# A fused attention and feed-forward kernel: the hidden tile of the seven-product blocks is taken from attention's four accumulator banks, and a probability buffer becomes a second copy of hs

## The chip, the cores and the metric

The kernel runs on one core of a Trainium2 chip. The metric is the time on the device in microseconds, the median of the runs shown. A core has five engines that matter here: TensorE (PE, matmuls, with its weight loads as PEld), VectorE (DVE), ScalarE (ACT), GpSimd (POOL) and SyncE (SP, which issues the transfers). Matmuls write into eight accumulator banks (PSUM), which VectorE and ScalarE read; this kernel's whole arrangement turns on who holds which bank.

## The reference

Eight heads of 64 and eight batches. Each of 512 local queries sees the 32 global keys and the local keys within 32 positions; each of 32 global queries sees all 544 keys. The 4608 rows that come out, 512 wide, go through a feed-forward pair with an ELU between:

```python
s_ll = where(abs(pos[:, None] - pos[None, :]) <= 32, scale * q_l @ k_l.T, -1e9)
a_l  = softmax(concat([scale * q_l @ k_g.T, s_ll]))        # local queries
out  = concat([softmax(scale * q_g @ k_all.T) @ v_all, a_l @ concat([v_g, v_l])])
x    = out.transpose(0, 2, 1, 3).reshape(4608, 512)
h    = x @ w_in                                            # 512 -> 2048
g    = where(h > 0, h, exp(min(h, 0)) - 1)
y    = g @ w_out                                           # 2048 -> 512
```

## The kernel before

**Two streams.** `attention()` and `ffn_stream()` are generators that are woven together: the last loop of `attn_ffn` draws stages of attention one by one and, after each, as many steps of the feed-forward stream as `pace` asks for. A `yield` ends a step; `tick` counts them, and `defer(n, fn)` writes an instruction into the program n ticks later. This gives the program's order. A planner then sorts the instructions into each engine's queue by that order as priority and by its own model of durations, and gives each tile of a pool a buffer as one comes free. On the chip each engine runs its queue in that fixed order and waits by semaphores.

**The banks.** Three pools divide the eight banks: `ps_h` (two, tiles h), `ps_o` (two, tiles acc) and `ps_a` (four, tiles pa).

**Attention.** A slot is one tile of 128 queries of four heads (64 such tiles, two groups g by four tiles t for each of eight batches), or the global queries of a batch and group (`stage_ga`). `stage_s` makes scores in two pa banks (L768), adds the mask and takes the extremum on VectorE (L779, into the buffer p), and defers the exponential (L785, ScalarE) and the scaling (L792, GpSimd). Two slots later `stage_t` transposes p (L808) into a pa bank, which line 810 copies out, and `stage_u` transposes global parts (L741, L744) into another, which lines 745 to 749 copy out. `stage_vv` multiplies by the values (L888, L821) into two banks for two tiles at a time; ScalarE (L896) and VectorE (L901) read them. From the third batch on, three slots after its first (`switch` in the code), a slot's stages come in the order T, S, U, V; before that S, V, T, U. The buffers p were a rotation of `LAGT + 1` = 3.

**Feed-forward.** The rows of x are taken in 18 blocks of 256. Weights and activations are split into a high and a low float16, and each product is three matmuls. Early blocks run in parts, as the weights' groups a to d become ready, with plain products (L445) in the acc banks. Once all weights are in (group f), a block's second layer is made by seven products of quarters in the manner of Strassen (`ffn2_seven`, L481), which need four accumulators for the eight pairs p of a block. Such a job carries a list, `seven`, which is None for the plain blocks.

`ffn1(job, p)` makes h for one pair: 24 matmuls (L322) into one bank. ScalarE reads h twice, as g (L331, Relu) and hs (L332, Copy), then takes the exponential of g (L333). VectorE joins g and hs (L340), for seven-product blocks four ticks later, and adds quarters (L354 to L356); ScalarE makes the high half gh (L359), VectorE the low half gl (L343). The second layer of a pair runs two pairs later (`LAG2`). At a block's end ScalarE evacuates the four accumulators (L491, L493). `ffn1_last` and `sums_of_last` do the same in smaller pieces for the very last pair.

**What sets h's bank before.** h comes from the two banks of `ps_h`. The first call of `ffn2_seven` takes four accumulators for the rest of the run: both acc, one h and one pa. From then on one bank is left for h and three for attention. When attention's stages are all issued (`alone`), every second h comes from `ps_a`. hs has one buffer.

Of the kernel before, what the change touches and what calls it, by code (L numbers as in the profile page):

```python
# [10 lines left out]
F32 = mybir.dt.float32  # L11
# [10 lines left out]
DM, DF = 512, 2048  # L22
P = 128
NT = SL // P
HQ = P // 2
KW = HQ + 3 * 32
# [34 lines left out]
def attn_ffn(ctx: ExitStack, tc: tile.TileContext, qT, qgT, kT, vT, vgT, vpT, w_in, w_out, mask, out):  # L61
# [35 lines left out]
            tick()  # L97

    lead = [True]
    alone = [False]  # L100


    msk = wts.tile([P, 3, KW], F32, name="msk")
# [7 lines left out]
    def clear(p):  # L111
        nc.gpsimd.memset(p[HQ:P, 0, :], 0.0)
        nc.gpsimd.memset(p[0:HQ, 1, :], 0.0)

    for p in ptw[:2]:
        clear(p)
    pkd = [wts.tile([P, P], F32, name=f"pk{i}") for i in range(2)]
    for p in pkd:
        nc.gpsimd.memset(p, 0.0)

# [182 lines left out]
    def ffn_stream():  # L303
# [3 lines left out]
        def ffn1(job, p):  # L307
            group, blk, xh, xl, sc, seven = job
            if (blk, p) == (order[-1], NP - 1):
                yield from ffn1_last(job, p)  # L310
                return
            state["h"] = not state.get("h")
            if alone[0] and state["h"]:
                h = ps_a.tile([P, 512], F32, name="pa").rearrange("p (j t) -> p j t", j=2)
            else:
                h = ps_h.tile([P, 2, BLK], F32, name="h")
            for j in range(2):
                f = slice((2 * p + j) * P, (2 * p + j + 1) * P)
                k = 0
                for c in range(NC):  # L320
                    for wt, xt in ((win[0], xh), (win[0], xl), (win[1], xh)):
                        nc.tensor.matmul(h[:, j, :], wt[:, c, f], xt[:, c, :], start=k == 0, stop=k == 11)  # L322
                        k += 1
                        if k == 6:
                            yield
                if j == 0:
                    yield
            g = ffn.tile([P, 2 * BLK], F32, name="g", bufs=2)
            hs = ffn.tile([P, 2 * BLK], F32, name="hs", bufs=1)
            hf = h.rearrange("p j t -> p (j t)")  # L330
            nc.scalar.activation(g, hf, AF.Relu, scale=sc[:, p:p + 1])  # L331
            nc.scalar.activation(hs, hf, AF.Copy, scale=sc[:, 2 * NP + 1 + p:2 * NP + 2 + p])  # L332
            nc.scalar.activation(g, g, AF.Exp, scale=-1.0)  # L333
            sg = sc[:, NP + p:NP + p + 1]
            shape = [P, 2 * BLK] if seven is None else [P, 7, P]
            gh = ffn.tile(shape, F16, name="gh", bufs=3)
            gl = ffn.tile(shape, F16, name="gl", bufs=3)

            def elu(out, *ins):
                nc.vector.scalar_tensor_tensor(out=out, in0=ins[0], scalar=-1.0, in1=ins[1], op0=ALU.add, op1=ALU.max)  # L340

            def low(dst, src, hi):
                nc.vector.scalar_tensor_tensor(out=dst, in0=src, scalar=sg, in1=hi, op0=ALU.mult, op1=ALU.subtract)  # L343

            def plain():
                elu(g, g, hs)
                nc.scalar.activation(gh, g, AF.Copy, scale=sg)
                defer(1, lambda: low(gl, g, gh))

            def parts():  # L350

                gx, q = quarters()
                elu(q, *(a.rearrange("p (a x) -> p a x", x=P) for a in (g, hs)))
                nc.vector.tensor_add(gx[:, 2:4, :], q[:, 0:2], q[:, 2:4])  # L354
                nc.vector.tensor_sub(gx[:, 5:7, :], q[:, 0:4:2], q[:, 1:4:2])
                nc.vector.tensor_add(gx[:, 0, :], q[:, 1], q[:, 2])  # L356

                def high():
                    nc.scalar.activation(gh, gx, AF.Copy, scale=sg)  # L359

                def lows():
                    low(gl, gx, gh)
                    seven.append(p)

                defer(2, high)
                defer(4, lows)

            defer(*(2, plain) if seven is None else (4, parts))
            pend.append((job, p, gh, gl))
            yield  # L370
# [7 lines left out]
        def ffn1_last(job, p):  # L378

            _, _, xh, xl, sc, seven = job  # L380
            g = ffn.tile([P, 2 * BLK], F32, name="g", bufs=2)
            hs = ffn.tile([P, 2 * BLK], F32, name="hs", bufs=1)
            s = new_x()[0].rearrange("p c (a x) -> p (c a) x", x=P)
            gh, gl = (ffn.tile([P, 7, P], F16, name=n, bufs=3) for n in ("gh", "gl"))
            q = g.rearrange("p (a x) -> p a x", x=P)
            sg = sc[:, NP + p:NP + p + 1]

            def parts(a, src):
                nc.scalar.activation(gh[:, a, :], src, AF.Copy, scale=sg)
                nc.vector.scalar_tensor_tensor(out=gl[:, a, :], in0=src, scalar=sg, in1=gh[:, a, :],  # L390
                                               op0=ALU.mult, op1=ALU.subtract)

            for j in range(2):
                h = ps_a.tile([P, 512], F32, name="pa")[:, 0:BLK]
                f = slice((2 * p + j) * P, (2 * p + j + 1) * P)
                k = 0
                for c in range(NC):
                    for wt, xt in ((win[0], xh), (win[0], xl), (win[1], xh)):
                        nc.tensor.matmul(h, wt[:, c, f], xt[:, c, :], start=k == 0, stop=k == 11)
                        k += 1  # L400
                        if k == 6:
                            yield
                gj, hj = (a[:, j * BLK:(j + 1) * BLK] for a in (g, hs))
                nc.scalar.activation(gj, h, AF.Relu, scale=sc[:, p:p + 1])
                nc.vector.tensor_scalar(hj, h, sc[:, 2 * NP + 1 + p:2 * NP + 2 + p], 1.0, ALU.mult, ALU.mult)
                nc.scalar.activation(gj, gj, AF.Exp, scale=-1.0)
                nc.vector.scalar_tensor_tensor(out=gj, in0=gj, scalar=-1.0, in1=hj, op0=ALU.add, op1=ALU.max)
                if j == 0:
                    nc.vector.tensor_sub(s[:, 5, :], q[:, 0], q[:, 1])
                    parts(1, q[:, 1])  # L410
                    parts(5, s[:, 5, :])
                    yield
            nc.vector.tensor_add(s[:, 2:4, :], q[:, 0:2], q[:, 2:4])
            parts(slice(2, 4), s[:, 2:4, :])
            nc.vector.tensor_sub(s[:, 6, :], q[:, 2], q[:, 3])
            nc.vector.tensor_add(s[:, 0, :], q[:, 1], q[:, 2])
            parts(4, q[:, 2])
            parts(0, s[:, 0, :])
            parts(6, s[:, 6, :])
            seven.append(p)  # L420
            pend.append((job, p, gh, gl))
            yield
# [38 lines left out]
        def ffn2_seven(blk, steps, sc, done):  # L461

            if "seven" not in state:
                state["seven"] = [ps_o.tile([P, DM], F32, name="acc"), ps_o.tile([P, DM], F32, name="acc"),
                                  ps_h.tile([P, 2, BLK], F32, name="h").rearrange("p a b -> p (a b)"),
                                  ps_a.tile([P, 512], F32, name="pa")]
            acc = state["seven"]
            oc = sc[:, 2 * NP:2 * NP + 1]
            final = blk == order[-1]
# [189 lines left out]
    def attention():  # L659
# [95 lines left out]
        def stage_s(st, g, t):  # L755
# [14 lines left out]
            mi = 0 if t == 0 else (2 if t == NT - 1 else 1)  # L770
            m = apool.tile([P, 4], F32, name="m", bufs=3)
            s = apool.tile([P, 2, 4], F32, name="sm", bufs=3)
            pp = apool.tile([P, 4, KW], F32, name="p", bufs=LAGT + 1)
            ps = [pp[:, i, :] for i in range(4)]
            np_[0] += 4
            for i in (0, 2, 1, 3):
# [171 lines left out]
        for i in range(n + LAGT + 1):  # L948
# [6 lines left out]
                load_values(s1)  # L955
            if i == switch:
                clear(ptw[2])
            for what in "SVTU" if i < switch else "TSUV":
                if what in "TU" and s1 and s1[0] == "l":
                    (stage_t if what == "T" else stage_u)(sts[s1[1]], *s1[2:])  # L960
                elif what == "V" and i < switch:
                    if s2 and s2[0] == "l":
                        stage_v(sts[s2[1]], *s2[2:])
                    if s0 and s0[1] < PAIRED:
                        load_values(s0)
                elif what == "V":
                    if pairs:
                        b, g, half = pairs.pop()
                        stage_vv(sts[b], g, half)
                    if s1 and s1[0] == "l" and s1[3] % 2 == 1:  # L970
                        pairs.append((s1[1], s1[2], s1[3] // 2))
                elif what == "S" and s0 and s0[0] == "g":
                    stage_ga(sts[s0[1]], s0[2])
                elif what == "S" and s0:
                    stage_s(sts[s0[1]], *s0[2:])
                yield
# [19 lines left out]
    for i, _ in enumerate(attention()):  # L996
# [10 lines left out]
        while done < want:  # L1007
# [3 lines left out]
            done += 1  # L1011
            convert(1)
            tick()
    alone[0] = True
    for _ in f:
        tick()
    drain()
# [52 lines left out]
```

## Time and profile before

| what | us |
|---|---|
| median of 3 runs (lowest to highest) | 968.35 (965.91 to 968.85) |
| the profiled execution, its own time | 968.7 |
| its span, first to last instruction | 966.9 |
| TensorE busy (mean granted clock 0.981) | 908.5 |
| VectorE busy | 739.7 |
| ScalarE busy | 662.7 |
| GpSimd busy | 271.2 |
| first h of a plain block (L322) | 84.6 |
| first and last start of a seven-product matmul (L481) | 332.9 and 961.1 |
| last matmuls of attention (L821) | 834.4 |

The table is read from the page, which gives engines as busy time, and from the views of single lines, which give first and last start. In the views below a row of the waits reads: engine and line that waited, what ended the wait, microseconds in total, times, the longest. A row of the timeline reads: start, duration, engine, line, operation, output and inputs, shapes, and in brackets the idle time of the engine before it and what ended that. A row of the groups ends with busy time, mean nanoseconds of one, and idle time of the engine ahead of them. A matmul's end is modelled and lies past the start of the next one, so a row's idle time is counted from there.

### The profile page before, as it was taken

Reading aid. Unit: us, or ns where it says so; the run is one execution under the profiler, and the core shown is the slowest. Engines: PE = TensorE matmul, PEld = TensorE weight load, DVE = VectorE, ACT = ScalarE, POOL = GpSimd, SP = SyncE. Lnnn points to the kernel's source line nnn. Section 1 sums busy time; section 2 is a strip of 40 time slices with the busy share of each in tenths; the row PEclk is TensorE's granted clock in tenths of the full one; section 3 lists DMA queues with packets and bytes.
Section 4 is the critical chain, followed back from the end, with each engine's and each line's share of the span. In section 5 each row is a group of like instructions: output and inputs, shape, how many; then the busy total and the mean of one; then the engine's idle time right before and its main releaser. Section 6 shows DMA issues by size and latency. Waiting matters only on the chain.

```text
span 966.9 us, 23599 instructions
## 1 busy us (share of the span) xinstructions
PE 908.5 (94%) x9216; PEld 725.6 (75%) x9216; DVE 739.7 (76%) x2033; ACT 662.7 (69%) x1568; POOL 271.2 (28%) x483
## 2 busy tenths in 40 slices
PE   5778988799999999999999999999999999999997
PEld 2546565466667788788888888888888788888886
DVE  4978999989957777768777777686777767676565
ACT  4767887776665777658676767676766767666564
POOL 3647193370532222122121212221322222110000
PEclk8899999999999999999999999999999999999999
DMA  7853765530343023101230123102310101000000
GB/s 268 287 173 129 254 221 197 185 118 37 120 138 119 25 99 100 47 26 45 100 124 26 45 78 123 45 27 83 115 48 25 45 24 34 1 23 23 1 23 22
DMA packets 41767, 87.61 MB, mean 91 GB/s; under 512 B 7736, under 2 KB 8888, under 8 KB 41656
## 3 DMA queue, kind: packets, MB, share of 16 engines
q1 hardware_dynamic: 41368, 85.85, 26.2%
q8 instruction: 72, 1.18, 0.5%
q14 instruction: 39, 0.32, 0.1%
q10 hardware_dynamic: 288, 0.26, 0.1%
HBM read 70.89 MB, written 15.20 MB: 89 GB/s over the span
## 4 chain that ended last, share of the span: by engine, by line
PE 59%; ACT 15%; DVE 15%; DMA 5%; issue 3%; POOL 2%; SPq 0%; DVEq 0%; ACTq 0%
PE h L322 23%; PE acc L481 10%; PE h L481 5%; PE acc L445 4%; PE pa L821 3%; PE pa L322 3%; ACT p L785 3%; PE pa L768 2%; DMA raw<-w_out 2%; PE pa L481 2%; ACT gh L359 2%; PE pa L808 2%; ACT g L331 2%; ACT hs L332 2%; DVE gl L343 2%
## 5 line engine op out<-in xcount | busy, mean ns | idle before, releaser
L322 PE MATMUL h<-xh,winh 128*128 128x256 f16 x984 | 269.3, 274 | 11.1 <-ACT hs L332 10.7
L322 PE MATMUL h<-xl,winh 128*128 128x256 f16 x984 | 269.0, 273 | 0.5 <-DVE xl L570 0.5
L322 PE MATMUL h<-xh,winl 128*128 128x256 f16 x984 | 269.0, 273 | 0.0
L322 PEld LDWEIGHTS <-winh 128*128 128x128 f16 x2160 | 209.2, 98 | 49.7 <-issue 19.2
L792 POOL TENSOR_SCALAR p<-p,sm 128x128 f32<-128x128 f32 x256 | 144.5, 580 | 319.4 <-DVE sm L790 198.3
L359 ACT ACTIVATE gh<-gx,xs 128x896 f16<-128x896 f32 x103 | 107.3, 1042 | 122.3 <-DVE gx L356 122.2
L343 DVE SCALAR_TENSOR_TENSOR gl<-gx,xs,gh 128x896 f16<-128x896 f32 x103 | 119.4, 1160 | 60.3 <-ACT gh L359 59.3
L481 PEld LDWEIGHTS <-gh 128*128 128x128 f16 x1456 | 139.6, 98 | 22.8 <-issue 6.2
L785 ACT ACTIVATE p<-p,m 128x160 f32<-128x160 f32 x256 | 106.6, 419 | 41.5 <-DVE m L779 41.3
L340 DVE SCALAR_TENSOR_TENSOR gx<-g,hs 128x512 f32<-128x512 f32 x103 | 72.8, 706 | 71.4 <-ACT g L333 70.0
L322 PEld LDWEIGHTS <-winl 128*128 128x128 f16 x1080 | 106.0, 98 | 14.0 <-issue 1.0
L331 ACT ACTIVATE g<-h,xs 128x512 f32<-128x512 f32 x123 | 84.0, 683 | 42.3 <-PE h L322 41.7
L481 PE MATMUL acc<-wouth,gh 128*128 128x256 f16 x312 | 85.2, 273 | 0.0
L333 ACT ACTIVATE g<-g 128x512 f32<-128x512 f32 x135 | 85.0, 630 | 0.0
L481 PE MATMUL acc<-woutl,gh 128*128 128x256 f16 x312 | 85.0, 273 | 0.0
L481 PE MATMUL acc<-wouth,gl 128*128 128x256 f16 x312 | 85.0, 273 | 0.0
L332 ACT ACTIVATE hs<-h,xs 128x512 f32<-128x512 f32 x123 | 83.8, 682 | 0.0
L481 PEld LDWEIGHTS <-gl 128*128 128x128 f16 x728 | 71.2, 98 | 9.3 <-DVE gl L343 1.0
L779 DVE CUSTOM_DVE_ANT_0 p<-pa,msk 128x160 f32<-128x160 f32 x228 | 61.1, 318 | 6.4 <-PE pa L768 6.2
L768 PE MATMUL pa<-k,q 64*64 64x160 f32 x912 | 51.4, 315 | 6.0 <-ACT ptg L749 5.3
L445 PE MATMUL acc<-wouth,gh 128*128 128x512 f16 x128 | 49.6, 388 | 7.3 <-DVE o L453 4.8
L808 PE MATMUL pa<-ident,p 128*128 128x128 f32 x256 | 43.9, 284 | 11.2 <-POOL p L792 9.6
(236 smaller groups left out, 1897.4 us busy)
## 6 DMA issues: line engine op xcount, KB each, us to landing
k<-kT SPq DMA_DIRECT2D x32, 640.0 KB, 5.1
v<-vT SPq DMA_DIRECT2D x64, 256.0 KB, 2.8
q<-qT SPq DMA_DIRECT2D x32, 256.0 KB, 5.5
raw<-w_in SPq DMA_DIRECT2D x8, 1024.0 KB, 7.0
raw<-w_out SPq DMA_DIRECT2D x8, 1024.0 KB, 6.1
out<-o SPq DMA_DIRECT2D x32, 256.0 KB, 2.3
od<-o SPq DMA_DIRECT2D x24, 256.0 KB, 3.1
o<-od SPq DMA_DIRECT2D x24, 256.0 KB, 2.8
```

Of the source, the lines that this page charges most:

```text
L322: nc.tensor.matmul(h[:, j, :], wt[:, c, f], xt[:, c, :], start=k == 0, stop=k == 11)
L331: nc.scalar.activation(g, hf, AF.Relu, scale=sc[:, p:p + 1])
L332: nc.scalar.activation(hs, hf, AF.Copy, scale=sc[:, 2 * NP + 1 + p:2 * NP + 2 + p])
L333: nc.scalar.activation(g, g, AF.Exp, scale=-1.0)
L340: nc.vector.scalar_tensor_tensor(out=out, in0=ins[0], scalar=-1.0, in1=ins[1], op0=ALU.add, op1=ALU.max)
L343: nc.vector.scalar_tensor_tensor(out=dst, in0=src, scalar=sg, in1=hi, op0=ALU.mult, op1=ALU.subtract)
L359: nc.scalar.activation(gh, gx, AF.Copy, scale=sg)
L445: nc.tensor.matmul(acc[t], gt[:, s], wt[:, f, :], start=p == first and j == 0 and k == 0, stop=p == last and j == 1 and k == 2)
L481: nc.tensor.matmul(cols, gt, w, start=p == 0 and k == 0, stop=last and k == len(todo) - 1, skip_group_check=True)
L768: nc.tensor.matmul(sp[r][half * HQ:(half + 1) * HQ, j * KW:(j + 1) * KW], q[rows, qs], k[rows, t, half, :], start=True, stop=True)
L785: nc.scalar.activation(ps[i], ps[i], AF.Exp, bias=m[:, i:i + 1], scale=-1.0, accum_out=s[:, 0, i:i + 1])
L792: nc.gpsimd.tensor_scalar(ps[i][:, 0:P], ps[i][:, 0:P], s[:, 1, i:i + 1], 1.0, ALU.mult, ALU.mult)
```

## The change

- h of a job with seven products comes from `ps_a`, always; h of a plain job comes from `ps_h`, always. The switch by `alone` and the alternation are gone.
- The four lasting accumulators of the seven products are both acc banks and both h banks; `ps_a` keeps its four.
- The three buffers of probabilities p become named tiles that are taken in turn (`turn`), and so does hs. At `switch` the oldest of the three leaves the rotation, and 512 of its 640 columns become a second hs. From there p has two buffers and hs has two; before it p has three and hs one.

```diff
-    alone = [False]
...
+    pps = [wts.tile([P, 4, KW], F32, name=f"p{i}") for i in range(LAGT + 1)]
+    hss = [wts.tile([P, 2 * BLK], F32, name="hs")]
+    turns = {"p": 0, "hs": 0}
+
+    def turn(name, tiles):
+        turns[name] += 1
+        return tiles[turns[name] % len(tiles)]
...
-            state["h"] = not state.get("h")
-            if alone[0] and state["h"]:
+            if seven is not None:
                 h = ps_a.tile([P, 512], F32, name="pa").rearrange("p (j t) -> p j t", j=2)
             else:
                 h = ps_h.tile([P, 2, BLK], F32, name="h")
...
-            hs = ffn.tile([P, 2 * BLK], F32, name="hs", bufs=1)
+            hs = turn("hs", hss)
...
-                state["seven"] = [ps_o.tile([P, DM], F32, name="acc"), ps_o.tile([P, DM], F32, name="acc"),
-                                  ps_h.tile([P, 2, BLK], F32, name="h").rearrange("p a b -> p (a b)"),
-                                  ps_a.tile([P, 512], F32, name="pa")]
+                state["seven"] = [ps_o.tile([P, DM], F32, name="acc") for _ in range(2)]
+                state["seven"] += [ps_h.tile([P, 2, BLK], F32, name="h").rearrange("p a b -> p (a b)") for _ in range(2)]
...
-            pp = apool.tile([P, 4, KW], F32, name="p", bufs=LAGT + 1)
+            pp = turn("p", pps)
...
             if i == switch:
                 clear(ptw[2])
+                k = turns["p"]
+                spare, *two = (pps[(k + i) % 3] for i in (1, 2, 3))
+                pps[:] = two if k % 2 else two[::-1]
+                hss.append(spare.rearrange("p h x -> p (h x)")[:, 0:2 * BLK])
...
-    alone[0] = True
```

More of the change, by code (lines that the diff above doesn't have):

```diff
@@ L381, in ffn1_last @@
             g = ffn.tile([P, 2 * BLK], F32, name="g", bufs=2)
-            hs = ffn.tile([P, 2 * BLK], F32, name="hs", bufs=1)
+            hs = turn("hs", hss)
             s = new_x()[0].rearrange("p c (a x) -> p (c a) x", x=P)
```

## The prediction

> **What bounds the kernel now.** I read the page first: the shares of the engines and the row of the granted clock. Then busy time by stage, cut where seven-product blocks begin (first matmul of line 481 at 333.0 us) and where attention has ended (its last matmuls run at 834 us).
>
> ```profile
> PE 908.5 (94%) x9216; PEld 725.6 (75%) x9216; DVE 739.7 (76%) x2033; ACT 662.7 (69%) x1568; POOL 271.2 (28%) x483
> ...
> PE   5778988799999999999999999999999999999997
> ...
> PEclk8899999999999999999999999999999999999999
> ```
> ```profile
> 0.00:180.00 180.00, 143.74 (x1366) 95.03 (x1367) 150.62 (x456) 130.92 (x347) 90.30 (x159) 0.93 0.65 220
> 180.00:333.00 153.00, 146.70 (x1252) 99.71 (x1251) 128.69 (x317) 102.69 (x248) 58.46 (x90) 0.97 0.29 98
> 333.00:837.00 504.00, 494.47 (x5473) 420.55 (x5471) 374.46 (x1087) 351.22 (x855) 116.09 (x227) 1.00 0.18 61
> 837.00:967.00 130.00, 123.62 (x1131) 110.35 (x1129) 85.91 (x176) 77.87 (x119) 6.36 (x9) 0.99 0.05 17
> ```
>
> The columns of the second view are the stretch, then busy time of TensorE, its weight loads, VectorE, ScalarE and GpSimd, and the granted clock. TensorE sets the time: in the stage that the change touches most, 333 to 837 us, it is busy 494.5 of 504 us at a clock of 1.00, and ScalarE and VectorE have about a quarter of it free. So the most that a better arrangement of banks can bring there is what TensorE still waits for. The waits, TensorE's alone, of the stage 180 to 333 us (two rows), of 333 to 837 (all four) and of 837 to 967:
>
> ```profile
> PE pa L768 <- ACT ptg L749: 3.0, 1, 3.0
> PE acc L445 <- DVE o L453: 2.1, 1, 2.1
> ```
> ```profile
> PE h L322 <- ACT hs L332: 7.7, 11, 1.4
> PE pa L741 <- DVE ptw L810: 0.8, 2, 0.6
> PE pa L768 <- DVE xglob L901: 0.4, 1, 0.4
> PE pa L888 <- ACT pg L719: 0.4, 1, 0.4
> ```
> ```profile
> PE h L481 <- DVE gl L343: 0.7, 1, 0.7
> ```
>
> One row carries the case. The one large wait of that stage is that of the first matmul of an h that waits for line 332, ScalarE's second read of the h before: in this stage one of the two h banks is an accumulator of the seven products, so h has a single bank. The largest of the eleven, in the timeline:
>
> ```profile
> 748.20 0.27 PE L322 MATMUL h<-xh,winh 128*128 128x256 f16 x1
> ...
> 750.53 0.48 ACT L493 ACTIVATE o<-pa,xs 128x256 f32<-128x256 f32 x1
> ...
> 752.25 0.27 ACT L749 COPY ptg<-pa 128x128 f32<-128x128 f32 x1
> 752.42 1.04 ACT L359 ACTIVATE gh<-gx,xs 128x896 f16<-128x896 f32 x1
> 753.36 0.68 ACT L331 ACTIVATE g<-h,xs 128x512 f32<-128x512 f32 x1
> 753.93 0.69 ACT L332 ACTIVATE hs<-h,xs 128x512 f32<-128x512 f32 x1
> ...
> 754.67 0.27 PE L322 MATMUL h<-xh,winh 128*128 128x256 f16 x1 [1.40 <-ACT hs L332]
> ...
> 756.07 0.77 PE L768 MATMUL pa<-k,q 64*64 64x160 f32 x16
> 756.97 1.04 ACT L359 ACTIVATE gh<-gx,xs 128x896 f16<-128x896 f32 x1 [1.83 <-DVE gx L356]
> ```
>
> The h begun at 748.20 is complete near 750.8, but ScalarE is behind at the end of a block (it has just evacuated the accumulators, L493) and reads it only from 753.36 to 754.62. TensorE stands still until then. At 756.97 ScalarE idles for 1.83 us again: its backlog is short, and a second bank would have bridged it.
>
> **The change part by part.**
>
> 1. *h of the seven-product blocks from the pool of four.* While attention runs, before: attention has three banks and h one. After: both share four. No instruction is added or removed. What goes is the wait above. The idle time is counted from the modelled end of the last matmul, 0.27 us after its start, while matmuls start 0.11 us apart (the next row: 24 in 2.62 us), so each wait is worth its row plus 0.16 us.
>
> ```profile
> 837.74 2.62 PE pa L322 x24
> 842.87 2.62 PE h L322 x24
> ```
>
> That makes 7.7 + 11 x 0.16 = 9.5 us, lying wholly on the path, since TensorE has hardly any other idle time before the end.
>
> What is late next? Around one of the eleven, at 435.07, the accumulators come next:
>
> ```profile
> 435.07 0.27 PE L322 MATMUL h<-xh,winh 128*128 128x256 f16 x1 [1.01 <-ACT hs L332]
> ...
> 438.50 0.69 ACT L491 ACTIVATE tmp<-h,xs 128x512 f32<-128x512 f32 x1
> ...
> 439.25 0.27 PE L481 MATMUL h<-wouth,gh 128*128 128x256 f16 x1
> ```
>
> The new block's product starts 0.06 us after line 491 has emptied its bank. Coming 1.17 us earlier it would wait for it, so this one (1.01 + 0.16 = 1.2 us) moves and isn't saved. Most others come after those products of their block or, like that at 754.67, right behind them, so nothing is moved onto that evacuation.
>
> Then the banks. Attention's own waits for its three banks are the rows of L741, L768 and L888 above: 1.6 us. With h sometimes holding two of four, attention has two or three. For an unchanged order of TensorE's stream and a bank always taken from those free longest, a shared pool never makes a tile wait longer than the split did: before, a tile could start when no h was out, or fewer than three of attention's; in either case fewer than four of the shared ones are out, and earlier starts free banks earlier. But the banks are dealt out ahead of time by a planner whose clock isn't the chip's, so I charge the same 1.6 us a second time; the bounds are 0 and the 20.6 us of the third rival.
>
> 2. *The accumulators in both h banks instead of one h bank and one of attention's.* They are taken once, at 333 us, when the last plain h's have to be out of both banks. TensorE showed no wait there. 0, with bounds of -0.7 to +0.7 us (the lone L481 wait above).
>
> 3. *After attention (837 to 967 us).* Before, h alternates between the two pools (the two rows of the chain above); after, it comes from the pool of four alone. No wait on line 332 stands there before, so 0; the cover is the alternation, which four banks replace.
>
> 4. *The second hs, from about 180 us on.* It would matter if line 332 waited for VectorE to have read the previous hs. It doesn't: its group on the page has 0.0 us of idle time ahead.
>
> ```profile
> L332 ACT ACTIVATE hs<-h,xs 128x512 f32<-128x512 f32 x123 | 83.8, 682 | 0.0
> ```
>
> So 0 by itself; what hides it is that VectorE's line 340 of one pair runs before the next h is complete. Without that cover h would be held longer and part 1 would lose. Bounds: -3.0 to +3.0 us, the largest single TensorE wait of the stage 180 to 333 (the row of L768), where the two copies already work on plain blocks.
>
> 5. *Two buffers of probabilities instead of three, from the same point.* Line 779 then writes the buffer that the transposes of line 808 read two tiles earlier. The closest that I found:
>
> ```profile
> 785.13 0.60 PE L808 MATMUL pa<-ident,p 128*128 128x128 f32 x4
> ...
> 788.23 0.33 DVE L779 CUSTOM_DVE_ANT_0 p<-pa,msk 128x160 f32<-128x160 f32 x1 [0.23 <-PE pa L768]
> ```
>
> The transposes are over at 785.73, the write starts at 788.23: 2.5 us to spare, because in TensorE's order the transposes of the tile two back stand ahead of the new scores, which the write needs anyway. 0; if that order were turned the write would wait on GpSimd's scaling, and the two score banks would be held longer. Before the switch three buffers rotate as ever; that they are named tiles rather than slots of a pool costs no instruction.
>
> The sum: -9.5 + 1.2 + 1.6 = -6.7 us. The profiled execution took 968.7 us with a span of 966.9, 0.35 above the median of 968.35. From its own time that is 962.0; from the median, 961.6. I say 961.6 us.
>
> **A rule weighed.** While TensorE waited at 754.67, the scores of line 768 stood behind it and started at 756.07, in their turn. The Trainium skill, "TensorE: Matmul & The Clock Gate", section on packing small matmuls, says that matmuls start and end in strict program order, without reordering; the trace agrees. By that rule a shared pool has a bad side: an attention tile that waits for a bank which a late h holds also stops the feed-forward matmuls behind it, and that is the third rival, priced from rows alone.
>
> **The rivals.**
>
> *The waits come back elsewhere (no change).* TensorE, ahead of ScalarE, would meet the accumulators' evacuation in every block, not in one, or the planner's new order would cost in the early stages what this one saves. For it: ScalarE is busy without a gap around 435, and 180 to 333 us has 6.3 us of idle TensorE that depends on order. Against it: the idle 1.83 us at 756.97. If two thirds of the 9.5 go: 968.35 - 3.2 + 1.6 = 966.8; between 965.5 and 971.
>
> *More than the sum (still faster).* Attention waits no more than now, the stall at 435 goes too, and the 3.0 us of L768 at 189 us falls to the second hs: 968.35 - 9.5 - 3.0 = 955.9.
>
> *Attention waits for banks (slower).* The place is the transposes of line 741, the first to want a bank after two banks of scores and one h are out:
>
> ```profile
> L741 PE MATMUL pa<-ident,pz x38: 272/273/328, 349.1 to 822.4; 128*128 128x128 f32 x38
> ```
>
> There are 38 of them between 333 and 837 us. If each wait costs what an h wait costs now, 9.5 / 11 = 0.86 us, it eats the gain from 11 of the 38 on; at 24 of 38 it is +20.6 - 9.5 = +11 us: 979. Against it: with three banks now only two waits of 0.8 us stand there.
>
> **How the numbers follow.** The runs shown lie within 0.3% (2.9 us), about what a measurement can tell from no change: faster is below 965.4, slower above 971.3. The forecast with its own range, 957 to 965, 0.58; more than the sum 0.06 (together faster 0.64); no change 0.21; slower 0.15. The range of 955.5 to 971 us takes in all but the third rival, and so leaves out 0.15.
>
> **What would show it.** In the trace after: the row of L322 waiting for line 332 gone or under 2 us between 333 and 837, a few short waits of pa tiles (under 4 us together), perhaps one of L481 on line 491; seven-product h's under the name pa from 333 us on; busy TensorE above 99% of that stage; line 332 still without idle time ahead; lines 808 and 779 as far apart as before. The stretch from 333.0 us to the end should shrink from 634 to about 627 us, with the start of the seven products where it was. Wrong would be: new waits of L741, L768 or L888 above 9 us together, L481 waiting for line 491 in most blocks, or a start of the seven products moved by more than 3 us.

## The result, and the profile after

The changed kernel took 962.13 us, the median of six runs (960.72 to 964.03), against 969.38 us for six runs of the kernel before. The ratio on record is 0.9934, with an interval of 0.9911 to 0.9957; dividing the two medians gives 0.9925, inside it. A second series beside three experiments gave 0.9928 (0.9910 to 0.9945). One run of the kernel before, among the 23 beside the last four experiments, took 5130 us and is left out of the ratios. The profiled execution has a span of 962.2 us.

In the changed kernel lines lie four or five further down: 322 is now 327, 332 is 337, 481 is 485, 491 is 495, 808 is 812. Busy time by stage, with the columns as before:

```profile
0.00:180.00 180.00, 148.61 (x1351) 98.05 (x1352) 146.44 (x446) 127.80 (x340) 87.01 (x157) 0.87 0.64 216
180.00:333.00 153.00, 147.54 (x1253) 99.22 (x1253) 131.21 (x322) 104.90 (x256) 61.45 (x89) 0.98 0.31 103
333.00:837.00 504.00, 499.67 (x5528) 426.66 (x5527) 377.84 (x1096) 353.83 (x861) 118.23 (x228) 1.00 0.18 61
```

From 333 to 837 us TensorE is now idle for 4.3 of 504 us, where it was 9.5, and has fitted 55 more matmuls in. What it still waits for in that stage, in the view of waits:

```profile
PE h L485 <- ACT tmp L495: 1.3, 1, 1.3
PE pa L892 <- ACT pg L723: 0.9, 2, 0.5
PE pa L745 <- DVE ptw L814: 0.8, 2, 0.6
PE pa L772 <- DVE xglob L905: 0.7, 1, 0.7
PE pa L892 <- issue: 0.4, 1, 0.4
```

The row of the first matmul of an h waiting for the second read of the h before (7.7 us, 11 times) is gone. A row that wasn't there has come: the new block's product (L485) waits once for the evacuation of its bank (L495). At the end of a block, where the longest stall stood, the timeline now reads:

```profile
746.12 0.27 PE L327 MATMUL pa<-xh,winh 128*128 128x256 f16 x1
...
748.66 0.48 ACT L497 ACTIVATE o<-h,xs 128x256 f32<-128x256 f32 x1
...
751.04 0.27 PE L327 MATMUL pa<-xh,winh 128*128 128x256 f16 x1
...
751.49 0.68 ACT L336 ACTIVATE g<-pa,xs 128x512 f32<-128x512 f32 x1
```

ScalarE reads the h begun at 746.12 only from 751.49, as late as before. But the next h starts at 751.04 in another bank, with no idle time in brackets.

The stage of the seven products can be measured apart from what goes before it: from its first matmul to the end of the span. The first start stands in the views of single lines (before, after):

```profile
L481 PE MATMUL acc<-wouth,gh x312: 272/273/283, 333.0 to 959.9; 128*128 128x256 f16 x156
```
```profile
L485 PE MATMUL acc<-wouth,gh x312: 272/273/283, 334.3 to 955.2; 128*128 128x256 f16 x156
```

966.9 - 333.0 = 633.9 us before, 962.2 - 334.3 = 627.9 us after. So the stage lost 6.0 us. The part ahead of it varied by more than the change moved it: in the second profile of the same changed kernel the seven products began at 331.3 us instead of 334.3. I use the stage's length below, beside the ratio.

### The profile page after: what moved, and what is told of

The parts are those of the page before. It is cut to its first block, busy times and chain, and to the rows that moved or that the text cites. A ratio compares the mean times of both kernels' runs of the same rounds, so it can differ in the third digit from the quotient of the medians.

```text
span 962.2 us, 23824 instructions
## 1 busy us (share of the span) xinstructions
PE 914.8 (95%) x9216; PEld 730.1 (76%) x9216; DVE 738.6 (77%) x2033; ACT 661.9 (69%) x1568; POOL 273.1 (28%) x483
## 4 chain that ended last, share of the span: by engine, by line
PE 67%; DVE 17%; ACT 8%; issue 3%; POOL 3%; DMA 1%; DVEq 0%; SPq 0%; ACTq 0%; POOLq 0%
PE pa L327 25%; PE acc L485 12%; PE h L485 9%; PE pa L825 4%; PE acc L450 3%; PE pa L772 3%; PE h L327 3%; PE pa L812 2%; ACT p L789 2%; DVE gl L348 2%; PE pa L892 2%; DVE cu L278 1%; POOL p L796 1%; PE pa L706 1%; DVE cu L196 1%
## 5 line engine op out<-in xcount | busy, mean ns | idle before, releaser
L327 PE MATMUL pa<-xh,winh 128*128 128x256 f16 x824 | 224.9, 273 | 0.1
L327 PE MATMUL pa<-xh,winl 128*128 128x256 f16 x824 | 224.6, 273 | 0.0
L327 PE MATMUL pa<-xl,winh 128*128 128x256 f16 x824 | 224.6, 273 | 0.0
L485 PEld LDWEIGHTS <-gh 128*128 128x128 f16 x1456 | 139.6, 98 | 24.0 <-issue 7.4
L336 ACT ACTIVATE g<-pa,xs 128x512 f32<-128x512 f32 x103 | 70.4, 683 | 24.1 <-PE pa L327 23.4
L485 PE MATMUL acc<-wouth,gh 128*128 128x256 f16 x312 | 85.2, 273 | 0.0
L485 PE MATMUL acc<-woutl,gh 128*128 128x256 f16 x312 | 85.0, 273 | 0.0
L485 PE MATMUL acc<-wouth,gl 128*128 128x256 f16 x312 | 85.0, 273 | 0.0
L485 PEld LDWEIGHTS <-gl 128*128 128x128 f16 x728 | 71.2, 98 | 9.2 <-DVE gl L348 1.0
L327 PE MATMUL h<-xh,winh 128*128 128x256 f16 x256 | 71.9, 282 | 4.1 <-ACT hs L337 3.1
L485 PE MATMUL h<-raw,gh 128*128 128x256 f16 x416 | 75.0, 273 | 0.0
L327 PE MATMUL h<-xl,winh 128*128 128x256 f16 x256 | 71.8, 281 | 0.7 <-DVE xl L574 0.7
L327 PE MATMUL h<-xh,winl 128*128 128x256 f16 x256 | 71.8, 281 | 0.0
L345 DVE SCALAR_TENSOR_TENSOR gx<-g,hs 128x512 f32<-128x512 f32 x51 | 35.9, 705 | 36.0 <-ACT g L338 35.7
```

Source lines behind the costliest of these rows:

```text
L485: nc.tensor.matmul(cols, gt, w, start=p == 0 and k == 0, stop=last and k == len(todo) - 1, skip_group_check=True)
```

## The experiments

The ratios are those on record; medians divided differ from them by up to 0.0015. The first three experiments and the second series ran on one chip, the last four on another, each group beside its own runs of the kernel before. The stage comes from one profile of each kernel.

| kernel | ratio to before (95%) | first seven-product matmul, us | span, us | stage, us |
|---|---|---|---|---|
| before | 1 | 333.0 | 966.9 | 633.9 |
| full change | 0.9934 (0.9911 to 0.9957) | 334.3 | 962.2 | 627.9 |
| full change again | 0.9928 (0.9910 to 0.9945) | 331.3 | 959.2 | 627.9 |
| banks alone | 0.9937 (0.9914 to 0.9959) | 329.9 | 957.9 | 628.0 |
| second hs, two p, banks as before | 0.9992 (0.9976 to 1.0008) | 331.0 | 965.0 | 634.0 |
| every second h from attention's pool | 1.0092 (1.0069 to 1.0116) | 333.1 | 977.6 | 644.5 |
| full change, pool of three banks | 1.0135 (1.0107 to 1.0162) | 329.5 | 979.7 | 650.2 |
| before, two evacuations on VectorE | 0.9998 (0.9979 to 1.0017) | 332.9 | 966.5 | 633.6 |
| before, added ScalarE work | 1.0053 (1.0031 to 1.0075) | 332.8 | 971.8 | 639.0 |
| full change, added ScalarE work | 0.9937 (0.9908 to 0.9966) | 334.6 | 963.6 | 629.0 |

My theory was the prediction's: a single h bank makes TensorE meet ScalarE's backlog at the end of a block, and a second bank bridges it; hs and the probability buffers do nothing. The first rival was that the second hs brings the gain, the second that the kind of sharing decides.

**The full change once more.**

> The changed kernel once more, beside the next three on one chip. Both theories: 0.993 of the kernel before (0.991 to 0.996). Its granted clock from 0 to 180 us, 0.87 in its first profile where the kernel before had 0.93, should differ from profile to profile if it is chance, and stay at 0.87 if the changed order causes it.

0.9928, and a stage of 627.9 us again. The clock from 0 to 180 us was 0.87 in this profile too, so it need not be chance. It isn't the banks: with the banks alone it is 0.91 there. It didn't move the start of the seven products in one direction (334.3 and 331.3 us, before 333.0), and I follow it no further.

**The banks alone.** hs keeps one copy and p three buffers:

```diff
             if i == switch:
                 clear(ptw[2])
                 k = turns["p"]
-                spare, *two = (pps[(k + i) % 3] for i in (1, 2, 3))
-                pps[:] = two if k % 2 else two[::-1]
-                hss.append(spare.rearrange("p h x -> p (h x)")[:, 0:2 * BLK])
```

> Only the banks: h of the seven-product blocks from the pool of four and both h banks as accumulators; hs keeps one copy and the probabilities three buffers. Theory (the whole gain is the second bank for h): 0.993 as the full change, no waits of L327 on line 337 between 333 and 837 us, and line 337 (the write of hs) still without idle time ahead of it. Rival (the second hs is what lets ScalarE free the bank, or lets the planner order it so): half the gain or less, 0.997 to 1.000, and waits for L345, VectorE's read of hs, ahead of line 337.

0.9937, and the stage is 628.0 us: the whole gain, by the banks. The waits of the stage are those of the full change, and one of 0.2 us:

```profile
PE h L485 <- ACT tmp L495: 1.3, 1, 1.3
...
PE pa L327 <- ACT hs L337: 0.2, 1, 0.2
```

The write of a single hs still has no idle time ahead of it (the group's last column), though h now runs ahead:

```profile
L337 ACT ACTIVATE hs<-pa,xs 128x512 f32<-128x512 f32 x103 | 70.2, 682 | 0.0
```

This run also settles whether a new order of the planner's brings the gain. Compared line by line, its trace and that of the kernel before have the same order of instructions on ScalarE and VectorE from start to end, and on TensorE but for one small matmul near 70 us. Only the banks differ.

**The buffers alone.** The full change with the old choice of banks: h from `ps_h` with the alternation at the end, accumulators from two acc, one h and one pa.

> Only the buffers: a second hs from the switch on, two buffers of probabilities, banks as before the change. Theory: 1.000 (0.998 to 1.002), with the eleven waits of h on the second read, 7.7 us, all still there. Rival (second hs): at least half the gain, 0.995 to 0.997. If two buffers of probabilities cost something that the banks hide in the full change, it shows here as over 1.002.

0.9992, and a stage of 634.0 us. The waits of h are all there, as 5.9 and 1.8 us; the first row names p because the second hs lies in a buffer of that name:

```profile
PE h L329 <- ACT p L339: 5.9, 9, 1.4
PE h L329 <- ACT hs L339: 1.8, 2, 1.0
```

With this the first rival has fallen: neither hs nor the two probability buffers gain or cost anything that can be measured.

**Every second h from attention's pool.** One line of the kernel before:

```diff
-            if alone[0] and state["h"]:
+            if (alone[0] or seven is not None) and state["h"]:
```

> The kernel before with one line changed: from the first seven-product block on, every second h comes from attention's three banks and the others from the one bank of its own (before, only after attention has ended). Theory: a second bank of any kind bridges ScalarE's backlog, so the waits of h on line 332 fall from 7.7 us to under 2; attention has three banks shared with every second h, so its own waits grow from 1.6 to about 3 us; 0.993 to 0.995. Rival (it is the pooling of all four that counts): the waits turn up at attention's tiles, over 6 us, and the time is 0.998 or more.

Here my theory failed as I had put it. The kernel became 0.9% slower than before, with the same banks and the accumulators where they were. The waits of h did vanish, but larger ones came to attention (the first five rows of the stage's waits):

```profile
PE pa L808 <- DVE xglob L901: 7.4, 4, 2.9
PE pa L808 <- DVE xg L901: 1.7, 2, 1.5
PE pa L741 <- ACT pg L719: 1.3, 3, 0.8
PE pa L888 <- ACT pg L719: 0.9, 2, 0.5
PE pa L888 <- ACT ptg L749: 0.8, 1, 0.8
```

The longest of them in the timeline:

```profile
554.95 1.54 PE L821 MATMUL pa<-ptw,v 128*64 128x96 f32 x32
...
555.84 0.67 ACT L332 ACTIVATE hs<-h,xs 128x512 f32<-128x512 f32 x1
...
556.76 0.27 PE L322 MATMUL pa<-xh,winh 128*128 128x256 f16 x1
...
561.10 0.35 DVE L901 TENSOR_REDUCE xglob<-pa 128x32 f32<-128x64 f32 x2
...
561.46 1.09 PE L808 MATMUL pa<-ident,p 128*128 128x128 f32 x4 [2.90 <-DVE xglob L901]
562.34 0.42 PE L322 MATMUL pa<-xh,winh 128*128 128x256 f16 x1
```

At 556.76 the values of two tiles hold two of attention's three banks, and the h whose turn it is takes the third. Its own bank was read for the last time up to 556.51, and stays empty because the turn says so. The transposes of line 808 now find no bank until VectorE has read the values (L901), 2.9 us later, and the half-made h stands behind them in TensorE's order. That is the prediction's third rival, at line 808 instead of 741. The planner also moved a few of TensorE's instructions in this stage (lines 741 to 744 twice, for one), so the run doesn't part the turns from that order wholly; ScalarE's and VectorE's order is that of the kernel before. All rows of the stage's waits sum to 14.6 us, where they were 9.3, and the clock took some 1.5 (last section); of the 10.6 us that the stage grew by, the remaining 3.8 are not broken down.

**The pool cut to three banks.**

```diff
-    ps_a = ctx.enter_context(tc.tile_pool(name="ps_a", bufs=4, space=PSUM))
+    ps_a = ctx.enter_context(tc.tile_pool(name="ps_a", bufs=3, space=PSUM))
```

> The changed kernel with attention's pool cut from four banks to three, so that one of the eight stays idle. Theory (the gain is a fourth bank that either side may take): by the traces attention's tiles and h together hold 2.1 banks on average, so three are short whenever two scores, two value banks or a late h meet; waits of pa tiles in the seven-product stage of 15 to 30 us and 1.010 to 1.025 of the kernel before. Rival (what counts is only that h isn't tied to one bank, whatever the number): under 5 us of waits and 0.993 to 0.998.

1.0135 and 17.9 us of waits of pa tiles, both within the expectation, and a stage of 650.2 us. The same rows lead the waits:

```profile
PE pa L812 <- DVE xglob L905: 7.6, 6, 2.6
PE pa L745 <- ACT pg L723: 2.4, 6, 1.0
PE pa L812 <- DVE xg L905: 2.1, 4, 1.2
```

Here too the rows (18.1 us in all) and the clock hold only part of the 16.3 us that the stage is longer than in the kernel before.

So, for attention and h together, the stage lasts as follows in us: three banks shared 650.2, three shared with every second h beside one private bank 644.5, three for attention and one for h 633.9, four shared 627.9.

**Two evacuations moved to VectorE, banks as before.**

```diff
-                        nc.scalar.activation(e[i].rearrange("p a b -> p (a b)"), acc[i], AF.Copy, scale=oc)
+                        er = e[i].rearrange("p a b -> p (a b)")
+                        if i:
+                            nc.vector.tensor_scalar(er, acc[i], oc, 1.0, ALU.mult, ALU.mult)
+                        else:
+                            nc.scalar.activation(er, acc[i], AF.Copy, scale=oc)
```

> The kernel before, with two of the three whole evacuations at a block's end (the second and third of line 491) moved from ScalarE to VectorE; banks as before. Theory (the waits of h are ScalarE's backlog at a block's end, met by a single bank): the backlog shrinks by 2 x 0.57 = 1.15 us, and the waits of h on line 332 between 333 and 837 us fall from 7.7 to 2 to 4 us; 0.994 to 0.998. Rival (the single bank stalls TensorE whatever ScalarE does): 6 us or more remain, 0.999 to 1.001.

The waits of h fell to 5.3 us in 7, less than my theory wanted and more than the rival allowed, while the time stayed, as the rival had it (0.9998, stage 633.6). Attention's waits grew from 1.6 to 2.9 us. And the lateness had moved:

```profile
PE h L322 <- ACT hs L332: 5.3, 7, 1.5
PE pa L892 <- ACT pg L723: 1.5, 3, 0.8
```
```profile
757.79 1.04 ACT L359 ACTIVATE gh<-gx,xs 128x896 f16<-128x896 f32 x1 [3.47 <-DVE gx L356]
759.98 0.66 ACT L331 ACTIVATE g<-h,xs 128x512 f32<-128x512 f32 x1
760.54 0.67 ACT L332 ACTIVATE hs<-h,xs 128x512 f32<-128x512 f32 x1
```

ScalarE is idle for 3.47 us, waiting for VectorE, which now evacuates; in the kernel before it waited 1.83 us at this place. The reads of h stand behind that wait in ScalarE's order, and the h at 761.26 waits 1.53 us for them. The h ahead of it had waited 0.99 us instead of 1.40 and started at 753.85 instead of 754.67, but the next reads came no sooner: 759.98 us, before 759.90. So "ScalarE's backlog" was too narrow at this block's end: it is the lateness of the chain ScalarE, VectorE, ScalarE, and work moved within that chain didn't shorten it. I followed this one block end; the others are not shown.

**Added ScalarE work, in the kernel before and in the changed one.**

```diff
                         nc.scalar.activation(o[0][:, 0:256], acc[i][:, 0:256], AF.Copy, scale=oc)
+                        for _ in range(6):
+                            nc.scalar.copy(scratch, e[2][:, 0, 0:32])
```

> The kernel before with six needless small copies on ScalarE behind the evacuations of each seven-product block (some 0.2 us each, 1.2 us in all, written to a scratch tile). Theory: a single h bank has nothing to bridge them, so the seven or eight waits behind block ends grow by about 1 us each: waits of h of 13 to 17 us, 1.006 to 1.010. Rival (the waits are of another origin): waits unchanged, under 9 us, and 0.999 to 1.002.

> The changed kernel with the same six needless copies. Theory: the second bank bridges them, because ScalarE idles again within two microseconds behind a block's end: waits of h under 2 us in the stage, 0.993 to 0.996 of the kernel before, so the two kernels with added copies lie some 1.3% apart instead of 0.7%. Rival (the four banks have no room to spare): the same growth as in the kernel before, 1.000 to 1.003.

The kernel before lost 0.5% (stage +5.1 us); the changed one's stage grew by 1.1 us, and its ratio to the kernel before is 0.9937, inside the interval of that without copies. They now lie 10 us apart in the stage instead of 6. The waits of h before grew less than I had written, from 7.7 to 9.9 us instead of 13 to 17, the ratio of 1.0053 lies just under my 1.006 to 1.010, and one wait for VectorE came to line 482. In the changed kernel there is no row of an h waiting for its bank above 0.5 us:

```profile
PE h L323 <- ACT hs L333: 9.9, 11, 2.3
PE acc L482 <- DVE gl L344: 0.9, 1, 0.9
```
```profile
PE pa L895 <- ACT pg L726: 2.0, 3, 1.1
PE h L486 <- ACT tmp L496: 1.3, 1, 1.3
PE pa L328 <- ACT p L338: 0.5, 1, 0.5
```

The copies overlap with their neighbours, so the six put ScalarE off by less than the 1.2 us that I had reckoned. At the block end that the prediction shows, the last evacuation and line 360 (359 before) now lie 2.76 us apart, before 1.89:

```profile
753.49 0.48 ACT L494 ACTIVATE o<-pa,xs 128x256 f32<-128x256 f32 x1
...
756.25 1.04 ACT L360 ACTIVATE gh<-gx,xs 128x896 f16<-128x896 f32 x1
```

ScalarE comes 0.87 us later there, and the wait of that h grew by just this, from 1.40 to 2.27 us. What the rows of waits don't hold of the 5.1 us is mostly the clock (the last section).

## Why the prediction was right, step by step

The forecast was 961.6 us, the measured median 962.13. That the two lie this close is luck: six runs of the changed kernel spread over 3.3 us, the median of the kernel before rose from 968.35 in three runs to 969.38 in six, and the start of the seven products varies by more than the error. The forecast of the stage is the better test: from 634 to about 627 us, it came out as 633.9 to 627.9, a loss of 6.0 us where the sum gave 6.7.

- *The wait of h goes (9.5 us).* Right: the row is gone, the banks alone do it, and added ScalarE work costs the kernel before but hardly the changed one.
- *One of the eleven only moves (1.2 us).* Right in place and size: the wait of L485 for L495 is 1.3 us and stands at 440.61, in the block end that the prediction named.
- *Attention's own waits (1.6 us charged).* By rows they went from 1.6 to 2.8 us (0.9 + 0.8 + 0.7 + 0.4), in six waits instead of four: 1.2 us, and 0.3 for the two more that are counted from modelled ends. The charge was right by size.
- *The sum.* All rows from 333 to 837 us: 9.3 us in 15 waits before, 4.1 in 7 after, so 5.2 + 8 x 0.16 = 6.5 us by waits; the stage lost 6.0. The 0.16 us is read from matmuls of h and carried over to the others.
- *Accumulators in other banks, the end, the second hs, two probability buffers: 0 each.* The last two are borne out by the experiment with the buffers alone, and by the equal stages of the full change and the banks alone. For the first two there is no experiment, but the rows agree: TensorE has no wait from 315 to 350 us, before or after, and behind 837 us only the 0.7 us for line 343 (348 after), as before. At the narrowest place the transposes and the write lie as far apart as before: 781.64 + 0.60 to 784.74, 2.5 us.

```profile
781.64 0.60 PE L812 MATMUL pa<-ident,p 128*128 128x128 f32 x4
...
784.74 0.32 DVE L783 CUSTOM_DVE_ANT_0 p<-pa,msk 128x160 f32<-128x160 f32 x1 [0.23 <-PE pa L772]
```

- *A shared pool is never worse than the split.* That held for the four that are free to either side, and so did its premise of an unchanged order of TensorE's stream, in the run with the banks alone. The argument needs a free choice among all four: the experiment with forced turns has the same four banks and is slower than both, in the way of the third rival, which the Trainium skill's rule on strict order ("TensorE: Matmul & The Clock Gate", on packing small matmuls) goes with. There the trace agrees again: the half-made h waited behind the transposes and went on at 562.34, in its turn.

What the prediction put too narrowly is the cause of the stall, "ScalarE is behind": moving its work to VectorE saved nothing that can be measured. The place and size of the cure didn't depend on it.

Open is what makes the start of the seven products vary from 329.5 to 334.6 us between profiles; it hides a few tenths of a per cent of any change.

## What to carry to other kernels

When the bounding engine waits for one tile's only bank while other banks stand empty, pool the banks rather than add a second one by turns: 6 us were gained by four banks free to either user, and 11 lost by a fixed alternation over the same four (some 1.5 of them by the clock, below). Price such a change from the row of the wait, add a matmul's modelled tail to each wait, and then look at what the freed engine runs into next: here one wait in eleven only moved to the evacuation behind it. Before moving work off a late engine, see whether it then waits for the engine that took the work: here the time stayed.

## What the runs showed of the hardware

A long stall costs more than its row. The four longest stalls of the seven-product stage, over all kernels, in the order of their length: with forced turns, in the kernel before with added ScalarE work, with three banks, and with forced turns again. The first three rows:

```profile
452.94 0.63 PE L808 MATMUL pa<-ident,p 128*128 128x128 f32 x4 [1.85 <-DVE xglob L901]
```
```profile
758.50 0.37 PE L323 MATMUL h<-xh,winh 128*128 128x256 f16 x1 [2.27 <-ACT hs L333]
```
```profile
560.68 1.08 PE L812 MATMUL pa<-ident,p 128*128 128x128 f32 x4 [2.58 <-DVE xglob L905]
```

and the 2.90 us at 561.46 shown above. Behind the first the granted clock stayed at 1.00; with the other three it fell. The stretches around the first, behind the 2.27 us, around the 2.58 us and around the end of the 2.90 us, with the clock as the third figure from the end:

```profile
448.30:451.71 3.41, 2.79 (x41) 2.24 (x37) 2.26 (x6) 2.98 (x9) 1.42 (x4) 1.00 0.47 109
451.71:455.13 3.42, 2.19 (x20) 2.04 (x21) 3.17 (x8) 1.04 (x1) 0.00 (x0) 1.00 0.13 50
453.00:457.00 4.00, 4.00 (x45) 3.31 (x46) 2.77 (x8) 2.16 (x4) 0.00 (x0) 1.00 0.00 0
```
```profile
758.00:762.00 4.00, 3.50 (x28) 2.38 (x27) 2.22 (x5) 2.00 (x3) 0.81 (x1) 0.57 0.18 69
```
```profile
556.00:560.20 4.20, 2.10 (x20) 1.63 (x18) 2.78 (x5) 1.82 (x4) 0.60 (x2) 1.00 0.40 125
560.20:563.60 3.40, 2.92 (x14) 2.33 (x15) 1.75 (x5) 0.00 (x0) 0.00 (x0) 0.51 0.00 0
563.60:568.00 4.40, 4.40 (x51) 3.61 (x50) 2.46 (x12) 3.28 (x10) 0.00 (x0) 0.99 0.00 0
```
```profile
560.94:564.36 3.42, 2.90 (x14) 2.30 (x15) 1.79 (x5) 0.00 (x0) 0.00 (x0) 0.50 0.00 0
```

The clock is about half for 3.4 us. Behind the 2.27 us all of it costs, 3.4 / 2 = 1.7 us on top of the stall. In the other two it began 0.4 and 0.5 us before the wait had ended, and cost TensorE half of the 2.9 us that it then ran, some 1.5 us. In the kernel before with added ScalarE work, the 1.7 us of the clock, the 2.2 us by which the waits of h grew and the 0.9 us of line 482 account for 4.8 of the 5.1 us that the work cost. In the kernel before and the changed one no wait of this stage is above 1.4 us, and they lost no clock, so the gain was the waits alone. The Trainium skill's page "TensorE: Matmul & The Clock Gate" (part on the clock gate) says that the clock falls to half after at least one idle window of some 3.4 us. The half clock agrees; a window idle throughout wasn't needed here.

The length of the wait alone doesn't decide, and the 1.85 us is no test of it. In these traces the half clock begins on a fixed grid of 3.41 us (with forced turns at 240.09 and 560.94 us, 94 steps apart) and lasts whole steps of it. The first two rows above are such steps: a border at 451.71 us divides the 1.85 us, and TensorE is idle for 0.6 us on one side and 1.2 on the other. Of each of the other three, 2.1 to 2.4 us fell within one step. In all ten traces, from 200 us on, each step at full clock with 2.06 us or more idle was followed by half clock, and none with 1.97 or less. Ahead of 200 us steps with 0.9 us of idle time were followed by it too, so idle time by these rows isn't the whole rule; what else counts there is open.
